# One written order for all nine chunks, and written places in SBUF and PSUM, for a local-attention and gated feed-forward kernel

## The chip, the cores and the metric

The kernel runs on one core of one Trainium2 chip, and the number that counts is the device time of one launch in microseconds. Before the change the median of three runs is 921.24 us (918.97, 921.24 and 921.79). One profiled execution was taken beside them; all rows quoted here are from it.

## The reference

The first half is attention of 8 batches with 8 heads of width 64: 512 local tokens that see the 32 global tokens and their neighbours within 32 places, and 32 global tokens that see all 544. The second half is a gated feed-forward layer on all 4608 tokens, with width 512 and hidden width 1536:

```python
a_l = sm(concat([s_lg, where(|i - j| <= 32, s_ll, -1e9)]));  out_l = a_l @ concat([v_g, v_l])
out_g = sm(scale * q_g @ concat([k_g, k_l]).T) @ concat([v_g, v_l])
x  = concat([out_g, out_l]).transpose(0, 2, 1, 3).reshape(4608, 512)
xn = x / sqrt(mean(x * x) + 1e-6) * rms_g
g, val = xn @ w_gate, xn @ w_val
out = (g * sigmoid(g) * val) @ w_out
```

## The kernel before, in words

The tokens are worked in nine chunks: chunks 0 to 7 are the 512 local tokens of a batch, chunk 8 the 256 global tokens of all batches. While TensorE (PE) does the feed-forward matmuls of one chunk, the attention of the next is done between them.

**Chunks 0 and 1** come first, with the weights still being made ready. `convert` (L451) loads a raw weight tile and splits it into two f16 parts on DVE and ACT, and chunk 0's feed-forward (`first_chunk`, L1747) waits for these tiles; its products with the first weights are jobs I, those with w_out are jobs O. The attention of both chunks is `local_unit` (L647): jobs L (load q and k), S (scores), M (minimum and exponent's argument, DVE), E (exponent, ACT), T (transposes), C (copies), A (product with v), X (normalise), Q (squares). Meanwhile `fold` (L1304, J, j, u, w) and `fold_out` (L1266) make sums of weight blocks and store them in DRAM (`wd`, `wa`, `wb`).

**Chunks 2 to 7** use those sums: `moe_pair` (L1360) does seven products of 2x2 blocks instead of eight, in the order 6, 1, 5, 7, 2, 3, 4, each 12 matmuls of 256 columns into a bank `pq`. Products 6, 1 and 5 begin banks; product 7 is added onto bank 6 once `s` was copied out of it, 2 onto 1, 3 onto 5 and 4 onto 6 again. So a product can wait for the DVE or ACT instruction (steps R) that read its bank. `moe_out` (L1547, O0 to O41) does the same with w_out into banks `pr`. Chunk 8 has plain `moe_f` products and `moe_out`. Attention is `local_halves` (L788, steps L, V, S, M, E, N, F, D, T, A, B, X, Y) and `global_unit` (L967): GS (scores), GM and GN (minimum and exponent), GT (transposes of the exponents `ge` into `gt`), GA (products). The weight tiles are read again for every chunk by `fetch` (L1339, tiles `wt`) and `fetch_out` (L1348, tiles `wu`): 512 KB each, on SP's DMA queue, which issues its transfers in order and waits at each until its buffer is free.

**Places.** SBUF tiles come from pools that rotate: tag "wf" has 12 buffers for `wt`, `wu`, `s`, `od` and the first weights, "wo" 7, "st" 6, "h" 6, "e" 4, "v" 4, "t" 3, "w" 3. The n-th tile of a tag takes the buffer of the n-12th (n-7th, ...), and waits for its readers. PSUM's eight banks are split the same way: "po" two, "pg" and "pv" one each, and four "pa" for attention (`attn_bank`, L446).

**Order.** All five engines are in a manual schedule (L1903): each runs its instructions as the program writes them. Chunk 0's jobs stand in a hand-made string ORDER (L40) and each is written out whole. For chunks 1 to 8 the instructions are recorded first and replayed in the order of a string per chunk, `_ORDER_1` to `_ORDER_8`, one chunk wholly behind the other. A piece "P12.0" is step P12's first run of instructions on one engine; a new piece begins where the engine changes, and at every instruction in steps R, t and n. Because replaying is done by a helper, every instruction of chunks 1 to 8 carries its line, L1929, in the profile:

```python
def write(engine, call):
    c, step, n, on = at_work
    if on and (on != engine or step[0] in "Rtn"):
        n += 1
...
for c, plan in plans.items():
    for name in orders.get(c, plan):
        for call in plan.pop(name) if c in orders else plan[name]:
            call()
```

Of the kernel before, what the change touches and what calls it, by code (L numbers as in the profile page):

```python
# [39 lines left out]
ORDER = """  # L40

# [22 lines left out]


_ORDER_1 = """
w0.0 S/0+1.0 M1/0+1.0 E1/0+1.0 w2.0 M3/0+1.0 E3/0+1.0 P0.0 N2/0+1.0 P1.0 N3/0+1.0 M2/0+1.0 E2/0+1.0
N1/0+1.0 M0/0+1.0 w3.0 w5.0 E0/0+1.0 N0/0+1.0 F0/0+1.0 P4.0 w6.0 F3/0+1.0 P5.0 R5.0 R6.0 P8.0 P9.0
F1/0+1.0 D1/0+1.0 R9.0 R1.0 F2/0+1.0 D3/0+1.0 D3/0+1.1 R10.0 P6.0 P7.0 R7.0 D0/0+1.0 D2/0+1.0
D2/0+1.1 R2.0 T2/0+1.0 P10.0 P11.0 w8.0 w9.0 P12.0 P2.0 T3/0+1.0 P3.0 D0/0+1.1 T0/0+1.0 D1/0+1.1  # L70
T1/0+1.0 A/0+1.0 B/0+1.0 P14.0 w12.0 Y/0+1.0 R3.0 R4.0 R5.1 w14.0 R11.0 R12.0 w1.0 X/0+1.0 R8.0 R9.1
GL/1+1.0 w15.0 P18.0 P16.0 P17.0 X/0+1.1 P19.0 Y/0+1.1 R17.0 R18.0 R19.0 R20.0 P13.0 R13.0 P32.0
P33.0 w18.0 GS/1+1.0 GM/1+1.0 Y/0+1.2 R13.1 GN/1+1.0 P24.0 P25.0 R14.0 w45.0 w20.0 w21.0 GM/1+1.1
GN/1+1.1 GT/1+1.0 GN/1+1.2 GT/1+1.2 GT/1+1.1 GT/1+1.3 P15.0 R15.0 L/2+1.0 S/2+1.0 R33.0 R34.0
M0/2+1.0 M2/2+1.0 N0/2+1.0 w49.1 N1/2+1.0 M3/2+1.0 N3/2+1.0 w24.0 E3/2+1.0 F3/2+1.0 P20.0 w17.0
R21.1 P40.0 D3/2+1.0 R25.0 R26.0 N2/2+1.0 R16.0 E2/2+1.0 R17.1 P21.0 R21.0 P22.0 P23.0 D3/2+1.1
R22.0 R23.0 T3/2+1.0 w26.0 w27.0 R24.0 R25.1 P26.0 P27.0 R27.0 R28.0 V/2+1.0 E0/2+1.0 F0/2+1.0
M1/2+1.0 F2/2+1.0 P28.0 P29.0 P41.0 R41.0 R29.1 X/0+1.2 w30.0 Y/0+1.3 P34.0 w23.0 P35.0 P30.0
D0/2+1.0 D0/2+1.1 R29.0 P31.0 R35.0 w44.0 P42.0 R30.0 R31.0 GV/1+1.0 R42.0 E1/2+1.0 GA/1+1.0 P43.0
F1/2+1.0 D1/2+1.0 D1/2+1.1 T1/2+1.0 w32.0 w33.0 L/0+2.0 R36.0 R37.1 P36.0 GD/1+1.0 P38.0 P66.0 R43.0  # L80
R44.0 D2/2+1.0 T0/2+1.0 D2/2+1.1 T2/2+1.0 w38.0 P37.0 R37.0 R38.0 w47.0 R45.1 w40.0 A/2+1.0 B/2+1.0
Y/2+1.1 X/2+1.0 X/2+1.1 w41.0 R32.0 P39.0 X/2+1.2 P44.0 P45.0 Y/2+1.0 X/2+1.3 Y/2+1.2 Y/2+1.3 R39.0
R40.0 R45.0 R46.0 R41.1 S/0+2.0 N0/0+2.0 M3/0+2.0 n53.0 P46.0 P47.0 n53.1 w46.0 R47.0 E3/0+2.0 n55.0
n55.1 n55.2 N1/0+2.0 n55.3 V/0+2.0 N2/0+2.0 n55.4 w48.0 n55.5 R33.1 N3/0+2.0 M2/0+2.0 E2/0+2.0
F2/0+2.0 P48.0 P67.0 P68.0 P49.0 P50.0 n55.6 n55.7 n55.8 n55.9 n55.10 w48.1 w35.0 P69.0 P70.0 n55.11
n55.12 n55.13 P51.0 P52.0 n56.0 R48.0 R49.0 P71.0 D2/0+2.0 M1/0+2.0 w46.1 n57.0 GX/1+1.0 w29.0
M0/0+2.0 D2/0+2.1 E0/0+2.0 n57.1 n64.1 w42.0 w49.0 w51.0 n65.0 P53.0 F3/0+2.0 n63.2 R71.0 w11.0
R53.0 F0/0+2.0 P54.0 P55.0 w54.0 w43.0 E1/0+2.0 F1/0+2.0 n56.1 n58.0 n58.1 R71.1 n62.1 n59.0 n59.2
P56.0 P57.0 D0/0+2.0 D0/0+2.1 n61.1 w56.0 P58.0 P59.0 n59.1 n63.0 P60.0 P61.0 GX/1+1.1 T2/0+2.0
w57.0 R53.1 D3/0+2.0 D3/0+2.1 D1/0+2.0 D1/0+2.1 T1/0+2.0 n64.0 n63.1 n60.0 n61.0 n65.1 T3/0+2.0  # L90
P62.0 P63.0 w59.0 P64.0 P65.0 R65.0 T0/0+2.0 R59.0 n62.0 R65.1 R59.1 n66.0
"""
# [187 lines left out]
def attention_moe_kernel(  # L280
# [363 lines left out]
    def local_unit(c, hp):  # L644
# [5 lines left out]
        def bank(name, tag):  # L650
            if not lead:
                return attn_bank(name)
# [1515 lines left out]
```

## Time and profile before

| | us |
|---|---|
| runs | 918.97, 921.24, 921.79 |
| span of the profiled execution, first to last instruction | 922.7 |
| PE busy | 878.8 (95%) |
| DVE busy | 724.5 (79%) |
| ACT busy | 556.3 (60%) |
| GpSimd (POOL) busy | 273.2 (30%) |
| mean granted TensorE clock | 0.980 of full speed |

The span is the profiled execution's own time; no other is given for it. It lies 1.46 us above the median of the runs. A busy time is the union of the times of an engine's instructions, so what is missing to the span is time in which the engine did nothing. In a list of waits each row is an engine's operation, what ended its idle time, the sum, the count and the longest. In the chain of waits each piece is a start, a duration and the engine and operation that the end of the program hung on at that moment.

### The profile page before, as it was taken

To read this page: it belongs to the slowest core of one execution; us is meant where nothing else is said; L and a number is where in the kernel's file an instruction comes from. 1 tells how busy PE (TensorE), PEld (TensorE's weight loads), DVE (VectorE), ACT (ScalarE), POOL (GpSimd) and SP (SyncE) were. 2 spreads that over 40 slices of the span, in tenths; PEclk is the share of its full clock that TensorE was granted. 3 is DMA by queue.
4 is the path that set the end of the run, shared out by engine and by line. 5 is a ranking of instruction groups with operands and counts; after the bars stand their busy time and mean duration, and the time that the engine had idled before them with its cause. 6 is when DMAs were issued, how large, how long until landed. Compare 5 with 4: busy or idle time off the path is not lost.

```text
span 922.7 us, 27756 instructions
## 1 busy us (share of the span) xinstructions
PE 878.8 (95%) x11430; PEld 671.4 (73%) x11430; DVE 724.5 (79%) x1831; ACT 556.3 (60%) x1341; POOL 273.2 (30%) x244
## 2 busy tenths in 40 slices
PE   5699989999999999999999999898999999999998
PEld 4644445544547886588888888787888888888887
DVE  6899998868796887877987888587887897777554
ACT  6899995636452755457565767466575862456132
POOL 0000000032435776306440244122520454133311
PEclk9699989999999999999999999999999999999999
DMA  9983615495377869686677769667876666888665
GB/s 337 405 301 106 192 47 173 130 333 174 90 248 243 274 206 300 194 257 233 206 258 263 245 222 293 198 208 243 265 250 223 206 222 244 247 246 273 215 232 191
DMA packets 101006, 212.03 MB, mean 230 GB/s; under 512 B 8080, under 2 KB 34448, under 8 KB 100880
## 3 DMA queue, kind: packets, MB, share of 16 engines
q1 hardware_dynamic: 100448, 209.94, 69.5%
q8 instruction: 89, 1.46, 0.6%
q10 hardware_dynamic: 432, 0.33, 0.1%
q14 instruction: 37, 0.30, 0.1%
HBM read 183.24 MB, written 27.00 MB: 228 GB/s over the span
## 4 chain that ended last, share of the span: by engine, by line
PE 40%; DVE 5%; DMA 3%; ACT 3%; issue 2%; POOL 1%; DVEq 0%; ACTq 0%; POOLq 0%; SPq 0%
PE pq L1929 20%; PE pr L1929 14%; PE p L1929 3%; DMA wt<-wd 2%; ACT e L1929 1%; PE a L1929 1%; DVE v L1929 1%; DMA wu<-wb 1%; DVE s L1929 1%; DVE u L1929 1%; POOL hs L1929 1%; POOL hu L1929 1%; PE s L1929 1%; ACT s L1929 1%; DVE t L1929 1%
## 5 line engine op out<-in xcount | busy, mean ns | idle before, releaser
L1929 PEld LDWEIGHTS <-wt 128*128 128x128 f16 x3312 | 322.7, 98 | 56.9 <-issue 11.1
L1929 PE MATMUL pq<-xh,wt 128*128 128x256 f16 x1152 | 206.6, 274 | 6.8 <-DMA wt<-wd 2.5
L1929 PE MATMUL pq<-ht,wt 128*128 128x256 f16 x1296 | 158.0, 274 | 2.1 <-POOL ht L1929 1.2
L1929 PE MATMUL pq<-xl,wt 128*128 128x256 f16 x576 | 157.8, 274 | 0.1
L1929 ACT ACTIVATE e<-e,sm 128x128 f32<-128x128 f32 x288 | 104.2, 390 | 27.8 <-DVE sm L1929 27.8
L1929 POOL TENSOR_TENSOR hu<-v,hu 128x256 f16<-128x256 f32 (+1 forms) x60 | 56.5, 958 | 177.6 <-ACT hu L1929 155.1
L1929 PE MATMUL pr<-wu,hs 128*128 128x256 f16 x792 | 92.4, 273 | 0.3 <-DVE hs L1929 0.3
L1929 POOL TENSOR_TENSOR e<-e,sm 128x512 f32<-128x512 f32 x24 | 27.7, 1162 | 205.3 <-DVE sm L1929 205.3
L1929 PEld LDWEIGHTS <-hs 128*128 128x128 f16 x792 | 77.4, 98 | 9.7 <-DVE hs L1929 0.6
L1929 POOL TENSOR_TENSOR hs<-u,hs 128x512 f16<-128x512 f32 x50 | 60.5, 1228 | 65.6 <-ACT hs L1929 37.9
L1929 PE MATMUL pr<-wu,hu 128*128 128x256 f16 x594 | 70.8, 273 | 1.0 <-DMA wu<-wb 0.6
L1929 DVE TENSOR_TENSOR s<-pq,s 128x512 f32<-128x512 f32 x66 | 44.9, 685 | 29.9 <-PE pq L1929 14.1
L1929 ACT ACTIVATE t<-u,half_inv 128x512 f32<-128x512 f32 x72 | 49.6, 717 | 27.0 <-DVE u L1929 23.0
L1929 DVE SCALAR_TENSOR_TENSOR t<-t,u 128x512 f32<-128x512 f32 x72 | 54.0, 758 | 14.4 <-ACT t L1929 14.3
L1929 ACT COPY s<-pq 128x512 f32<-128x512 f32 x72 | 41.3, 580 | 38.3 <-DVE s L1929 18.2
L1929 PEld LDWEIGHTS <-hu 128*128 128x128 f16 x594 | 57.6, 98 | 8.6 <-DMA wu<-wb 0.9
L1929 DVE TENSOR_TENSOR v<-pq,s 128x512 f32<-128x512 f32 x72 | 49.0, 683 | 18.6 <-PE pq L1929 14.8
L1929 PE MATMUL po<-wo,h 128*128 128x512 f16 x288 | 63.4, 379 | 0.0
L1651 PE MATMUL p<-xh,wf 128*128 128x512 f16 x192 | 58.8, 379 | 3.1 <-DVE t L1763 1.2
L1929 PE MATMUL p<-xh,wf 128*128 128x512 f16 x192 | 59.8, 385 | 0.5 <-DVE t L1929 0.5
L1651 PEld LDWEIGHTS <-wf 128*128 128x128 f16 x288 | 27.7, 98 | 37.0 <-issue 3.1
L1929 PEld LDWEIGHTS <-wf 128*128 128x128 f16 x288 | 27.8, 99 | 34.6 <-issue 2.9
(380 smaller groups left out, 1704.7 us busy)
## 6 DMA issues: line engine op xcount, KB each, us to landing
wt<-wd SPq DMA_DIRECT2D x120, 512.0 KB, 5.3
wu<-wb SPq DMA_DIRECT2D x36, 512.0 KB, 5.3
wr<-in_w_in_dram SPq DMA_DIRECT2D x24, 512.0 KB, 8.7
wu<-wa SPq DMA_DIRECT2D x24, 512.0 KB, 4.7
k<-in_qkb_dram SPq DMA_DIRECT2D x24, 448.0 KB, 6.5
gkq<-in_gkq_dram SPq DMA_DIRECT2D x16, 576.0 KB, 7.1
wt<-wd SPq DMA_DIRECT2D x36, 256.0 KB, 4.2
v<-in_vb_dram SPq DMA_DIRECT2D x24, 352.0 KB, 5.6
```

Of the source, the lines that this page charges most:

```text
L1651: nc.tensor.matmul(ps[:, :n], rows[:, a, o : o + P], ch[z][k][:, :n], start=(k == 0 and i == 0), stop=(k == NK - 1 and i == 2),)
L1929: return lambda *a, **k: write(self.engine, lambda: call(*a, **k))
```

## The change

Chunk 0 is now recorded like the others (`JOBS` only says which jobs there are), and one string ORDER of 3692 pieces "chunk:step.n" holds all nine chunks, so that steps of different chunks can be written in any order. Every instruction on DVE and GpSimd is now a piece of its own, in all chunks. No instruction goes to another engine, and the arithmetic and the transfers stay as they were.

The pools that rotate are gone. SBUF is 43 pages of 1024 words and 8 wide ones of 1152 words in each partition, allocated once, and PSUM is eight banks. A string PAGES names the page (and the quarter of it) of each of 1169 tiles, and a string BANKS the bank of each of 444 uses. Tiles under 256 words get a place of their own for the whole run. A tile's first writer now waits for the last readers of whatever the strings put in that place before it.

```diff
-for name in ORDER.split():
-    job.pop(name)()
-plans = {c: {} for c in range(1, NCH)}
-at_work = [1, "", 0, ""]
+plan = {}
+at_work = [0, "", 0, ""]
...
-        if on and (on != engine or step[0] in "Rtn"):
+        if on and (on != engine or engine in ("vector", "gpsimd") or c and step[0] in "Rtn"):
             n += 1
...
+for name in JOBS.split():
+    doing(0, name)
+    job.pop(name)()
...
-    orders = {c: names.split() for c, names in ORDERS.items()}
-    for c, plan in plans.items():
-        for name in orders.get(c, plan):
-            for call in plan.pop(name) if c in orders else plan[name]:
-                call()
+    for name in ORDER.split() or list(plan):
+        for call in plan.pop(name):
+            call()
...
+    page = [con.tile([P, 1024], F32, tag=f"page{i}", name=f"page{i}") for i in range(NPAGE)]
+    wide = [con.tile([P, 1152], F32, tag=f"wide{i}", name=f"wide{i}") for i in range(NWIDE)]
+    banks = [psum.tile([P, 512], F32, tag=f"bank{i}", name=f"bank{i}") for i in range(8)]
+    def tile_of(shape, dt, name):
+        n = int(np.prod(shape[1:])) * (2 if dt in (F16, BF16) else 4) // 4
+        if n < 256:
...
+            return con.tile(shape, dt, tag=tag, name=tag)
+        at = next(page_at)
...
+    def bank_of(name):
+        return banks[int(next(bank_at))]
...
-        t = pool.tile([P, 2, 2, 2, HT], F16, tag="wf", bufs=NF, name=f"wt{c}_{g}{i}")
+        t = tile_of([P, 2, 2, 2, HT], F16, f"wt{c}_{g}{i}")
...
-            ps = [[attn_bank(f"gs{b}{h}{z}") for z in range(2)] for h in range(2)]
+            ps = [[bank_of(f"gs{b}{h}{z}") for z in range(2)] for h in range(2)]
...
-    nc = bacc.Bacc("TRN2", target_bir_lowering=False, num_devices=1)
+    nc = bacc.Bacc("TRN2", target_bir_lowering=False, num_devices=1, dynamic_dma_scratch_size=2048)
```

The start of the order before, and after:

```
z0 L0 S0 M0.0 M0.1 L1 S1 M1.0 E0.0 M1.1 E0.1 T0.1 T0.0 W0 m0 s0 E1.0 C0.0 z1 l0 g0 L2 S2 M2.1 T1.0
0:L2.0 0:L0.0 0:S0.0 0:M0.0.0 0:M0.0.3 0:M0.0.1 0:M0.0.2 0:E0.0.0 0:z0.0 0:M0.1.2 0:L3.0 0:W1.0
```

## Rows read from the trace of the kernel before

**Rows 1.** The page: busy time of each engine.

```profile
PE 878.8 (95%) x11430; PEld 671.4 (73%) x11430; DVE 724.5 (79%) x1831; ACT 556.3 (60%) x1341; POOL 273.2 (30%) x244
```

**Rows 2.** Stages: start:end, length, PE, PEld, DVE, ACT, POOL busy, clock, DMA, GB/s.

```profile
0.00:44.10 44.10, 27.27 (x602) 23.54 (x603) 32.52 (x149) 34.00 (x100) 0.20 (x4) 0.77 0.98 370
44.10:129.10 85.00, 77.37 (x719) 39.48 (x719) 82.23 (x195) 81.49 (x141) 0.00 (x0) 0.98 0.54 183
129.10:172.40 43.30, 43.30 (x513) 24.22 (x511) 36.98 (x85) 26.69 (x66) 0.00 (x0) 0.97 0.32 109
172.40:910.50 738.10, 722.23 (x9528) 576.68 (x9523) 570.47 (x1401) 413.63 (x1034) 272.24 (x239) 0.99 0.73 236
910.50:922.70 12.20, 8.68 (x78) 7.53 (x78) 2.27 (x5) 0.48 (x2) 0.72 (x1) 1.00 0.27 101
```

**Rows 3.** Waits of PE from 129.1 us to the end: sum, times, longest.

```profile
PE pq L1929 <- DMA wt<-wd: 3.4, 4, 2.2
PE gt L1929 <- ACT ge L1929: 2.6, 2, 2.3
PE a L1929 <- issue: 2.4, 2, 2.2
PE pq L1929 <- DVE s L1929: 1.9, 4, 1.2
PE pq L1929 <- ACT u L1929: 1.5, 1, 1.5
PE pq L1929 <- POOL ht L1929: 1.2, 1, 1.2
PE pq L1929 <- DVE u L1929: 0.6, 1, 0.6
PE pr L1929 <- DMA wu<-wb: 0.6, 1, 0.6
```

**Rows 4.** Four stretches of 3.4 us, as rows 2: the granted clock beside matmuls done.

```profile
589.40:592.80 3.40, 3.40 (x18) 2.36 (x17) 0.30 (x1) 1.32 (x4) 0.00 (x0) 0.50 0.99 266
...
596.20:599.60 3.40, 3.40 (x34) 3.05 (x32) 1.36 (x4) 0.59 (x1) 0.00 (x0) 1.00 0.17 64
626.90:630.30 3.40, 3.16 (x15) 2.24 (x16) 0.31 (x1) 3.35 (x14) 0.51 (x1) 0.50 0.99 295
210.50:213.90 3.40, 3.40 (x34) 1.43 (x39) 0.86 (x3) 1.54 (x4) 0.00 (x0) 0.50 0.57 160
```

**Rows 5.** Chain of waits, two places: start us, us, what.

```profile
498.07 9.17 PE pq L1929 x84
...
621.09 2.43 POOL hs L1929 x2
623.53 3.56 DMA wt<-wd
627.14 8.27 PE pq L1929 x60
```

**Rows 6.** Timeline of PE, 583 to 588 us: [idle before <- releaser].

```profile
583.46 2.22 PE L1929 MATMUL a<-et,v 32*64 32x256 f32 x139
...
587.86 0.42 PE L1929 MATMUL a<-et,v 32*64 32x64 f32 x21 [2.18 <-issue]
```

**Rows 7.** The page: the DMA queue of instructions (packets, MB, share).

```profile
q8 instruction: 89, 1.46, 0.6%
```

**Rows 8.** Waits of SP's DMA queue, whole span: the largest.

```profile
SPq L1929 <- PE pq L1929: 142.3, 65, 9.9
```

**Rows 9.** Waits of PE, 0 to 129.1 us: the two largest.

```profile
PE x00t L1110 <- DVE dg L1104: 6.3, 1, 6.3
PE s L688 <- DMA k<-in_qk_dram: 6.1, 1, 6.1
```

**Rows 10.** Waits of DVE, 8 to 125 us: for PE's attention products.

```profile
DVE x L757 <- PE a L746: 2.2, 1, 2.2
```

**Rows 11.** DVE's t<-t,u, both inputs in SBUF: ns least/median/most.

```profile
L1929 DVE SCALAR_TENSOR_TENSOR t<-t,u x72: 650/685/1625, 298.3 to 847.8; 128x512 f32<-128x512 f32 x72
```

More of the change, by code (lines that the diff above doesn't have):

```diff
@@ L72 @@
[L72 to L77, printed above, removed]
@@ L645, in local_unit @@
         u = c * (H // 2) + hp
[L646 removed]
         st = {}
         xt = chunks[c]["x"]
[L650 to L664 removed]
+        def load():
+            q = tile_of([P, SL], F32, f"q{u}")
+            k = tile_of([P, 1024], F32, f"k{u}")[:, :KU]
             nc.sync.dma_start(q, qk[u, :, :SL])
@@ L669, in load_v @@
         def load_v():
-            tag = "wf" if lead and hp >= 2 else "v"
             v = st["v"] = [
-                pool.tile([P, 1024], F32, tag=tag, bufs=NF if tag == "wf" else 4, name=f"v{u}{i}")
+                tile_of([P, 1024], F32, f"v{u}{i}")
                 for i in range(2)
@@ L679, in scores @@
             q, k = st["q"], st["k"]
-            st["sm"] = pool.tile([P, 3, 8], F32, tag="sm", bufs=SMB, name=f"sm{u}")
-            ps = st["ps"] = [bank(f"s{u}{h}", "pa") for h in range(2)]
+            st["sm"] = tile_of([P, 3, 8], F32, f"sm{u}")
+            ps = st["ps"] = [bank_of(f"s{u}{h}") for h in range(2)]
             for i in range(NT):
@@ L769, in sums @@
             if hp == 0:
-                chunks[c]["ss"] = pool.tile([P, 4, NK], F32, tag="ss", name=f"ss{c}")
+                chunks[c]["ss"] = tile_of([P, 4, NK], F32, f"ss{c}")
             nc.vector.tensor_reduce(
@@ L794, in load @@
             if w == 0:
-                late["mask"] = con.tile([P, 6 * P], F32, tag="mask", name="maskb")
+                late["mask"] = tile_of([P, 6 * P], F32, "maskb")
                 nc.sync.dma_start(late["mask"], maskb)
@@ L864, in scores @@
         def scores():
-            st["sm"] = pool.tile([P, 3, 16], F32, tag="sm2", bufs=2, name=f"sm{u}")
-            ps = [[attn_bank(f"s{u}{x}{bk}") for bk in range(2)] for x in range(2)]
+            st["sm"] = tile_of([P, 3, 16], F32, f"sm{u}")
+            ps = [[bank_of(f"s{u}{x}{bk}") for bk in range(2)] for x in range(2)]
             st["s"] = ps
@@ L885, in scores @@
             st["et"] = [
-                pool.tile([P, 1088], F32, tag="k", name=f"et{u}{x}") for x in range(2)
+                tile_of([P, 1088], F32, f"et{u}{x}") for x in range(2)
             ]
@@ L909, in values @@
             if ms[0] == blocks[0]:
-                st["a"] = [attn_bank(f"a{u}{p}") for p in range(4)]
+                st["a"] = [bank_of(f"a{u}{p}") for p in range(4)]
             ps = st["a"]
@@ L931, in values, with taken @@
                         )
-        def take(z):
+        def taken(z):
             x = x_part(c, 2 * hp + z)
@@ L1231, in high @@
                 pair = [
-                    pool.tile([P, 512], F16, tag=s, bufs=4, name=f"{s}{c}{p}") for s in ("xh", "xl")
+                    tile_of([P, 512], F16, f"{s}{c}{p}") for s in ("xh", "xl")
                 ]
@@ L1362, in moe_pair @@
         st = {}
-        bank = {6: "po", 1: "pg", 5: "pv"}
+        own = (6, 1, 5)
         onto = {7: 6, 4: 6, 3: 5, 2: 1}
@@ L1367, in products @@
         def products(n, p):
-            if p in bank:
-                st["ps", p] = psum.tile(
-                    [P, 512], F32, tag=bank[p], bufs=2 if bank[p] == "po" else 1, name=f"pq{p}_{g}"
-                )
+            if p in own:
+                st["ps", p] = bank_of(f"pq{p}_{g}")
             ps = st["ps", p] = st["ps", onto.get(p, p)]
@@ L1374, in products @@
             hi, lo = ch["op"][p]
-            first = p in bank
+            first = p in own
             for j in range(2):
@@ L1513, in sums, with both @@
                 nc.vector.tensor_tensor(s[:, 1, 1], v[:, 1, 0], s[:, 0, 1], ALU.subtract)
-        def both(name, tag, bufs):
-            t = pool.tile([P, 2, 1024], F16, tag=tag, bufs=bufs, name=f"{name}{g}")
+        def both(name):
+            t = tile_of([P, 2, 1024], F16, f"{name}{g}")
             t = t[:, :, : 4 * w].rearrange("p a (j n) -> p a j n", j=2)
```

805 lines of the change are left out of this document (477 added, 328 removed), and 9 rows, old and new, of the table BANKS.

## The prediction

> **What bounds the kernel now.** I read the busy times first: TensorE (PE) is busy 878.8 us, DVE 724.5 [rows 1]. No matmul goes away, so the floor of any reordering is about PE's work, and only PE's idle time and its stretches at half clock can be won. The view by stage says where the idle time lies [rows 2]: 44.1 - 27.27 = 16.8 us before the first feed-forward matmul; 85.0 - 77.37 = 7.6 us up to chunk 0's first O product; nothing in the next 43.3 us; 738.1 - 722.23 = 15.9 us over chunks 1 to 8; 12.2 - 8.68 = 3.5 us in the tail, nearly all behind the last matmul. The first 129 us have another bound: DVE is busy 82.23 and ACT 81.49 of 85 us, making weights and attention ready [rows 2], so PE waits there because of work, not order.
>
> For the 15.9 us I read what ended PE's waits [rows 3]. No cause is large: weight tiles 3.4 + 0.6, the global units' exponents 2.6, no visible releaser 2.4, and copies out of a bank that the next product is added onto (s, u) 1.9 + 1.5 + 0.6, POOL 1.2. The eight rows hold 14.2 us. The stretches of 3.4 us show what they cost besides [rows 4]: with the granted clock at 1.00 (2.4 GHz) one did 34 matmuls, at 0.50 (1.2 GHz) one did 18, so it lost 16 x 0.10 = 1.6 us. There are three such stretches after 172 us, each behind a PE wait of over 2 us (210.5 follows the exponents' wait, 589.4 the one without releaser, 626.9 a weight tile's). What order can win in chunks 1 to 8 is thus 15.9 + 3 x 1.6 = 20.7 us.
>
> **The change part by part.** The sum is made against the profiled span of 922.7 us, 1.46 above the median of 921.24; I subtract from the median.
>
> *Weight tiles.* The chain shows how such a wait comes about [rows 5]: POOL's `hs` ended, only then SP issued the `wt` load into that buffer, 3.56 us later the product began, at half clock. The queue spends its time like this: 142.3 us of waiting for `pq` products alone [rows 8]. I counted in both orders the PE work between a tile's fetch and its first use, a 256-column matmul at 9.17/84 = 0.109 us [rows 5]. For `wt` of chunks 3 to 7 the mean grows from 8 to 13 us to 39 to 54 us, for `wu` from 4 to 11 us to 31 to 58 us. Tiles with under 8 us of lead fall from 109 to 31. Of 3.4 + 0.6 us I take off the share of those that go, 78 of 109: 2.9. With the half-clock stretch: -4.5 us. Bounds: -5.6 (all), and 0 if the page is not free when the fetch stands at the queue's head.
>
> *Exponents before their transposes.* GS to GT had 2.6 us of PE work in three of eight units, and now has 5.2 or more in all, up to 51. I take off 2.6 + 1.6 = -4.2 us; bounds -4.2 and -2.1 (one of the two waits stays).
>
> *The wait without releaser.* Before it PE ran 139 small matmuls, each with a weight load of its own, in 2.22 us, and then stood 2.18 us [rows 6]. The queue that carries instructions moved 89 packets of 1.46 MB / 89 = 16 KB [rows 7]; PE has 2 x 11430 instructions [rows 1], and 22860 / 89 = 257 of them a packet. So 278 instructions outran a packet here. The text of the change cannot show whether the boundaries now fall elsewhere: dense groups that stand side by side (A with B, GT with GT) number 12 before and 12 after. Bounds 0 and -(2.4 + 1.6) = -4.0; only one of 12 such groups stalled, so one cannot count on it either way: -2.0, the middle. [...]
>
> *Products added onto a bank.* The work between a product and the one onto its bank (144 pairs in chunks 2 to 7) grows from 4.4 to 6.4 us in the mean; the least is one product, 1.3 us, in both. DVE's s, ACT's u and DVE's u cost 4.0 us now; halved, -2.0. POOL's `ht` 1.2: halved, -0.6. Bounds 0 and -5.2.
>
> *Port.* DVE's t<-t,u takes 0.685 us but up to 1.625 [rows 11], only in operations with two SBUF inputs, as if POOL held it off. DVE is not the bound after 172 us (570 of 738 us busy [rows 2]), so calmer pieces gain nothing beyond the copies above: 0.
>
> *The first 129 us.* Unit 2's q and k are loaded ahead of unit 0's: 640 KB at the 370 GB/s of this stage [rows 2], 1.7 us, on top of the 6.1 us that the first scores wait for k [rows 9]; if the first scores are of unit 0, nearly all of it is paid. DVE's wait for attention products, 2.2 us [rows 10], can be covered by conversion work now that single instructions can be moved. DVE's work ahead of the first O product falls from 123.6 to 121.6 us, ACT's rises from 121.3 to 123.7. Conversion of one weight tile is moved ahead of the norm of chunk 0 (the 6.3 us at x00t [rows 9]), so that DVE's counted work ahead of the first feed-forward matmul rises from 37.0 to 40.4 us and ACT's from 38.6 to 42.2; it is spared later. I take 0; bounds -4 (both engines' savings) and +4 (load 1.7 and ACT's 2.4).
>
> *Chunk 0 to 1, tail.* PE is never idle from 129.1 to 172.4 us [rows 2]: a new mixture there gains 0. The tail hangs on the last product and its store: 0.
>
> *New waits.* The new order has its own least distances (31 short leads, 1.3 us between products). One stall like the weight tile's, 2.2 + 1.6 = 3.8 us, is what a single bad place costs; bounds 0 and, in this case, 3.8; I take half, +1.9.
>
> Sum: -4.5 - 4.2 - 2.0 - 2.0 - 0.6 + 0 + 1.9 = -11.4; 921.24 - 11.4 = 909.8 us.
>
> **The rivals.** *B, the whole idle time goes.* If every wait of chunks 1 to 8 and its half-clock stretch disappears (20.7) and DVE's 2.2 us at the start too, the time is 921.24 - 22.9 = 898. For it: the leads are four times as long; against it: the least distances did not change.
>
> *C, others take their place.* PE's waits are eight different causes of 0.6 to 3.4 us; take one off and the next engine is late: DVE does 570 us in the same 738. If long leads hold pages that attention needs, its waits grow as the weights' shrink, and the time stays at 921.
>
> *D, slower: SP's queue blocks.* The queue issues in order. An early fetch that waits for a page holds everything behind it, and behind it stand the 31 tiles with under 8 us of lead and the loads of q, k and v. The longest wait at `pq` is already 9.9 us [rows 8]. Each tile so held stalls PE by the 2.2 us of 627.14 and 1.6 us of half clock, 3.8 in all. Against the -11.4 three of them make no difference, from four it is slower (925.0), with six it is 932.6. Against it: a wait of the queue hurts only if it exceeds the lead of a tile behind it, and 78 of 109 short leads are gone.
>
> **How the numbers follow.** Forecast 909.8 with 0.50: its own ends come from the bounds: tiles and instruction wait in full and no new wait give 921.24 - 5.6 - 4.2 - 4.0 - 2.0 - 0.6 = 904.8; one exponent wait left (+2.1), the whole new stall (+1.9) and the start's +4 give 917.8. B has 0.15, C 0.14, D 0.21. A measurement of this kernel tells about 0.3% from no change, 918.5 to 924.0. Faster: A and B, 0.65; same: C, 0.14; slower: D, 0.21. The range runs from 899, at the upper edge of B, to 929, between four and six stalls of D; outside it lie about half of B and half of D, 0.2.
>
> **What would show it.** Right: PE's idle time over chunks 1 to 8 falls from 15.9 to about 7 us, the waits for `wt` and `gt` fall to under 1 us each, at most one stretch at clock 0.50 stands after 172 us, and the first O product begins within 4 us of 129.1. B: idle under 2 us. C: idle still near 15 us, with other names. D: waits of PE for `wt` or `wu` of over 2 us, four or more, behind long waits in SP's queue. The forecast is wrong as a whole if the first stage ends later than 134 us or earlier than 124, for then DVE and ACT's order mattered, which I priced at nothing.

## The result and the profile after

The changed kernel takes 904.52 us (median of four runs, 902.98 to 905.86) against 920.29 us of the kernel before on the same chip: a ratio of 0.9821 with a 95% interval from 0.9802 to 0.9841, 15.8 us less. The two profiled executions are 922.7 and 903.1 us long, 19.6 us apart. The one of before was a long one. In the 48 other executions of that kernel that were timed beside the runs below, the time is 2.1 to 2.2 us more than the span, so the time of this one was some 924.8 us (an estimate): about 3.6 us above the median of 921.24, and not 1.46 as the span alone makes it. Its mean granted clock is 0.980, where those 48 have 0.987 in the median. The one of after is near its median (904.84 us, span 903.1, clock 0.989). So what is read from this pair can be up to some 4 us more than what the medians show.

Since tiles are now parts of pages, the names of tiles in the profile after are `page`, `wide` and `bank`, and the helper's line is L2088. The page of the kernel after, busy time of each engine (it answers to [rows 1]):

```profile
PE 869.2 (96%) x11430; PEld 668.4 (74%) x11430; DVE 701.2 (78%) x1831; ACT 553.8 (61%) x1341; POOL 273.8 (30%) x244
```

The same count of instructions on every engine, and PE is busy 9.6 us less: it does the same matmuls for less time at half clock (mean granted clock 0.989, before 0.980). The stages of after [rows 2], cut at its own first O product (123.2 us) and its own last stretch:

```profile
44.10:123.20 79.10, 78.34 (x748) 42.69 (x749) 77.93 (x184) 78.35 (x138) 0.00 (x0) 0.98 0.63 222
123.20:892.00 768.80, 760.99 (x10045) 600.34 (x10045) 591.23 (x1501) 441.62 (x1104) 271.33 (x235) 1.00 0.70 231
892.00:903.10 11.10, 7.56 (x69) 6.47 (x67) 2.58 (x7) 0.95 (x2) 2.26 (x5) 1.00 0.12 47
```

The kernel before from its first O product to the same matmul near the end:

```profile
129.10:910.50 781.40, 765.53 (x10036) 600.90 (x10034) 607.45 (x1485) 440.31 (x1100) 272.24 (x239) 0.99 0.71 229
```

So the 19.6 us are two pieces. Up to the first O product 129.10 - 123.25 = 5.9 us are won. From there to the end 13.7 us are won, 8.0 us of PE's idle time (from 15.9 to 7.8 us up to the last stretch, 3.5 us in both last stretches) and 5.7 us of PE's own. The last stretch of after is shorter only because the cut leaves it 69 matmuls, and that of before 78. PE's own 5.7 us go with the clock: no stretch at 0.50 is left behind 123 us in this execution. The kernel before had four behind 128 us: three are in [rows 4], the fourth, and one more ahead of it, are these:

```profile
121.80:125.10 3.30, 3.30 (x128) 2.89 (x112) 2.10 (x14) 3.30 (x11) 0.00 (x0) 0.50 0.03 5
128.60:132.00 3.40, 3.40 (x11) 1.50 (x10) 3.33 (x7) 2.80 (x6) 0.00 (x0) 0.50 0.18 71
```

How many such stretches there are differs from execution to execution (the mean granted clock of the 48 lies between 0.980 and 0.993), as the section on half clock below shows too, so the 5.7 us cannot be put down to the order alone.

The waits of PE in the kernel after, from the first O product on, answer to [rows 3]:

```profile
PE bank L2088 <- issue: 5.4, 7, 1.1
PE bank L2088 <- ACT page L2088: 1.3, 3, 0.6
PE bank L2088 <- DVE nt L2088: 0.4, 2, 0.3
PE bank L2088 <- POOL page L2088: 0.4, 1, 0.4
PE bank L2088 <- DVE sm L2088: 0.2, 1, 0.2
```

The reader is to see what is missing: no wait for a transfer, none for exponents. What is left has no visible releaser, and no wait is longer than 1.1 us. In the first stage the two waits of [rows 9] still stand; the one for k is longer (8.6 us, before 6.1):

```profile
PE bank L2088 <- DMA page<-in_qk_dram: 8.6, 1, 8.6
PE bank L2088 <- DVE page L2088: 6.8, 2, 6.6
```

### The profile page after: what moved, and what is told of

It reads as the page before. It is cut to its first block, busy times and chain, and to the rows that moved or that the text cites. A ratio compares the mean times of both kernels' runs of the same rounds, so it can differ in the third digit from the quotient of the medians.

```text
span 903.1 us, 27864 instructions
## 1 busy us (share of the span) xinstructions
PE 869.2 (96%) x11430; PEld 668.4 (74%) x11430; DVE 701.2 (78%) x1831; ACT 553.8 (61%) x1341; POOL 273.8 (30%) x244
## 3 DMA queue, kind: packets, MB, share of 16 engines
q8 instruction: 89, 1.46, 0.7%
## 5 line engine op out<-in xcount | busy, mean ns | idle before, releaser
L2088 PE MATMUL bank<-page,page 128*128 128x256 f16 (+6 forms) x8212 | 714.6, 281 | 24.8 <-DMA page<-in_qk_dram 8.6
L2088 PEld LDWEIGHTS <-page 128*128 128x128 f16 (+1 forms) x5472 | 525.0, 98 | 175.5 <-issue 11.4
L2088 POOL TENSOR_TENSOR page<-page,page 128x512 f16<-128x512 f32 (+5 forms) x177 | 200.5, 1152 | 361.4 <-ACT page L2088 319.8
L2088 ACT CAST page<-page 128x512 f16<-128x512 f32 (+1 forms) x156 | 121.2, 797 | 93.4 <-DVE page L2088 72.5
L2088 ACT COPY page<-bank 128x512 f32<-128x512 f32 (+3 forms) x163 | 85.1, 543 | 115.7 <-PE bank L2088 103.1
L2088 DVE TENSOR_TENSOR page<-bank,page 128x512 f32<-128x512 f32 x155 | 104.7, 685 | 59.2 <-PE bank L2088 48.7
L2088 ACT ACTIVATE page<-page,sm 128x128 f32<-128x128 f32 x352 | 128.8, 389 | 24.4 <-DVE sm L2088 21.7
L2088 DVE TENSOR_TENSOR page<-page,page 128x256 f32<-128x256 f32 (+5 forms) x171 | 102.4, 609 | 11.0 <-ACT page L2088 8.7
L2088 PE MATMUL bank<-wide,page 32*64 32x96 f32 (+6 forms) x2268 | 103.5, 271 | 1.3 <-issue 1.3
L2088 POOL TENSOR_TENSOR page<-page,sm 128x512 f32<-128x512 f32 x24 | 27.9, 1176 | 214.4 <-DVE sm L2088 200.5
L2088 ACT ACTIVATE page<-page 128x512 f32<-128x512 f32 (+2 forms) x94 | 77.6, 894 | 10.2 <-DVE page L2088 5.5
L2088 PEld LDWEIGHTS bank<-page,page 64*32 64x32 f32 (+4 forms) x3232 | 58.4, 116 | 29.5 <-issue 14.7
L2088 DVE CUSTOM_DVE_ANT_0 page<-bank,page 128x128 f32<-128x128 f32 x256 | 62.0, 284 | 19.9 <-PE bank L2088 16.5
L2088 DVE TENSOR_TENSOR page<-page 128x256 f32<-128x256 f32 (+3 forms) x127 | 69.3, 556 | 1.2
L2088 DVE SCALAR_TENSOR_TENSOR page<-page,page 128x512 f32<-128x512 f32 x65 | 46.9, 734 | 12.6 <-ACT page L2088 12.4
L2088 DVE SCALAR_TENSOR_TENSOR page<-page,c_h,page 128x512 f32<-128x512 f32 x69 | 51.7, 769 | 0.9
L2088 ACT ACTIVATE page<-page,half_inv 128x512 f32<-128x512 f32 x65 | 44.6, 716 | 12.8 <-DVE page L2088 11.5
L2088 ACT ACTIVATION_READ_ACCUMULATOR page<-page,sm 128x1 f32 x256 | 48.0, 187 | 0.0
L2088 PE MATMUL bank<-page,wide 128*128 128x256 f16 x330 | 41.7, 273 | 0.6 <-ACT page L2088 0.6
L2088 ACT ACTIVATE page<-bank,half_inv 128x512 f32<-128x512 f32 (+1 forms) x36 | 21.7, 610 | 31.7 <-PE bank L2088 31.7
L2088 DVE STREAM_TRANSPOSE wide<-page 128x512 f32<-128x512 f32 x48 | 32.6, 696 | 6.5 <-POOL page L2088 6.5
L2088 PEld LDWEIGHTS <-wide 128*128 128x128 f16 x330 | 31.9, 98 | 5.1 <-issue 1.0
```

The lines of the kernel that those rows point to most:

```text
L2088: return lambda *a, **k: write(self.engine, lambda: call(*a, **k))
```

## The experiments

Each run has its own kernel before on the same chip; ratios are to that.

### What sets the first O product

The chain to the first O product goes through the scale of w_out (steps K), which needs all six of its weights converted on DVE and ACT. The order before had eight pieces of chunk 0's hidden values ahead of it (c4 to c7, casts on ACT, and r4 to r7, subtractions on DVE), the new order has them behind. Here they are put back, and one page is changed so that they fit:

```diff
-0:K0.1 ... 0:c4.0 0:c5.0 0:c6.0 0:O0.1.0 ... 0:c7.0 ... 0:r5.0 ... 0:r4.0 0:r7.0 ... 0:r6.0
+0:c4.0 0:r4.0 0:c5.0 0:r5.0 0:c6.0 0:r6.0 0:c7.0 0:r7.0 0:K0.1 ... 0:O0.1.0
```

> The changed kernel with c4 to c7 and r4 to r7 of chunk 0 (ACT's casts and DVE's subtractions for the hidden values of 4 to 7) put ahead of the norm of w_out (step K0's second piece), as the order before had them. Theory DVE (what DVE and ACT have to do ahead of the last weights' scale sets the first O product): 4 x 0.69 us on DVE come ahead, so the first O product begins 2 to 3 us later (125.2 to 126.3 us), and the end as much, 906 to 908 us. Rival PE (the first O product came sooner because transposes and products of the attention no longer stand in a row in front of it): it begins within 0.7 us of 123.25 and the time stays within 1 us.

906.78 us, ratio 0.9859 (0.9827 to 0.9892). Timeline of PE in this run:

```profile
123.62 0.59 PE L2088 MATMUL bank<-kk,ones 128*128 128x1 f32 x2 [2.86 <-DVE kk L2088]
...
128.10 1.49 PE L2088 MATMUL bank<-page,page 128*128 128x512 f16 x3
```

and of the changed kernel at the same place:

```profile
120.35 0.28 PE L2088 MATMUL bank<-kk,ones 128*128 128x1 f32 x2
...
123.25 1.02 PE L2088 MATMUL bank<-page,page 128*128 128x512 f16 x4 [0.15 <-ACT page L2088]
```

DVE in this run, ahead of the scale's first step (`qo`):

```profile
119.43 1.29 DVE L2088 TENSOR_TENSOR wide<-page,wide 128x512 f16<-128x512 f32 x2 [0.73 <-ACT wide L2088]
120.64 1.29 DVE L2088 TENSOR_TENSOR page<-page,page 128x512 f16<-128x512 f32 x2
121.85 0.16 DVE L2088 TENSOR_TENSOR qo<-hs 128x6 f32<-128x6 f32 x1
```

The four subtractions and the wait for ACT's cast ahead of them take 0.73 + 2.42 = 3.15 us, and the matmul of the scale, which waits 2.86 us for DVE's `kk`, comes 3.3 us later than in the changed kernel. The first O product comes 4.9 us later, more than expected: behind the wait the clock was 0.50 for two stretches, so that the way from the scale to the O product took 4.5 us in place of 2.9. In the kernel before the scale's matmul came 4.9 us later than in the changed one:

```profile
125.25 0.38 PE L626 MATMUL nrm<-kk,ones 128*128 128x1 f32 x2
```

So the eight pieces are 3.3 of those 4.9 us; what the rest is, no run shows. For the first O product the theory DVE holds, with half clock on top. The end moved less, by 3.6 us between the profiled executions (906.7 and 903.1 us) and by 2.3 between the medians, and the intervals of the two ratios overlap.

The loads of unit 0 ahead of those of unit 2:

```diff
-0:L2.0 0:L0.0 0:S0.0
+0:L0.0 0:L2.0 0:S0.0
```

> The changed kernel with the loads of unit 0 ahead of those of unit 2 again. Theory: the first scores begin 1.7 to 2.5 us sooner (6.1 to 6.9 us in place of 8.6) and, since DVE is packed from there to the first O product, that product and the end come 1.5 to 2.5 us sooner: 901.5 to 903 us. Rival: unit 2's scores are the ones that DVE then waits for, and the first O product stays within 0.7 us of 123.25.

902.80 us, ratio 0.9816 (0.9788 to 0.9844): 1.7 us less than the changed kernel and in the range of the theory, but the intervals overlap. The first O product came at 120.89 us, 2.4 us sooner, as the theory has it, and the profiled execution ended 2.0 us sooner (901.1 us). Near 515 us a new wait stands:

```profile
515.68 4.57 PE L2088 MATMUL bank<-page,page 128*128 128x256 f16 x25 [2.62 <-DMA page<-wd]
```

The tile was issued at 511.87, because SP's queue had waited for a store:

```profile
SPq L2088 <- PE bank L2088: 10.8, 3, 5.3
SPq L2088 <- DMA out_dram<-page: 5.5, 1, 5.5
```

and the clock fell behind it:

```profile
516.50:519.90 3.40, 3.40 (x19) 2.38 (x17) 0.59 (x2) 0.68 (x1) 2.64 (x3) 0.51 0.20 74
```

The page of this weight tile had held an output tile, and the load could not start until the store of that tile was through. So one of 1169 places was changed on top of the loads:

```diff
-24a 7c 20a w2 w1 27a 29a 10c W5a W4a 22a 15a 15c 1a 4a W4a 11a 0a 15a 4c 24a 28a 25a 11a 36a 23a 4a
+24a 7c 20a w2 w1 27a 29a 10c W5a W4a 22a 15a 15c W2a 4a W4a 11a 0a 15a 4c 24a 28a 25a 11a 36a 23a 4a
```

> The run with unit 0 loaded first, and one page changed: the weight tile of chunk 4 that TensorE waited 2.6 us for there (its page held an output tile, so SP waited 5.5 us for that tile's store to land) goes to wide page 2, which is free for long. Theory QUEUE (that one wait and the stretch at clock 0.50 behind it gave back the 2.4 us that the earlier start had won): no wait of TensorE for wd over 1 us, no stretch at 0.50 after 172 us, 898 to 901 us. Rival: the 2.4 us are lost elsewhere, 901.5 to 904 us.

901.03 us, ratio 0.9774 (0.9754 to 0.9794), 3.5 us less than the changed kernel and the fastest of this study. The wait is gone (all waits for `wd` after 123 us: 0.7 us), no stretch at 0.50 is left behind 172 us, so the theory QUEUE holds for the cause of that wait. Its price is not shown: the first O product lay at 122.1 us in this execution and the span was 900.2 us, the median is 1.8 us below that of the run before it and just above what was expected, and the intervals of the two ratios touch. Nor had the wait given back the whole 2.4 us, since that run had already ended 2.0 us sooner than the changed kernel.

### Leads and distances, as the prediction counted them

The fetches of 162 pieces were moved back to about 9 us of PE work ahead of their use, for example

```diff
-6:w52.0 7:w11.0 8:w48.0 6:t43.1
+6:w52.0 7:w11.0 6:t43.1
...
-8:R48.4 8:R50.0 8:O12.0
+8:R48.4 8:R50.0 8:w48.0 8:O12.0
```

> The changed kernel with each fetch of a weight tile for chunks 3 to 8 moved back in the order to about 9 us of TensorE work ahead of its first use (162 pieces moved; the mean lead was 44 us). Theory LEADS (long leads are what took the weight tiles' waits away): waits of TensorE for the loads come back, 3 to 6 us in all, with at least one stretch at clock 0.50 after 172 us; 908 to 913 us. Rival: with the new order of the other steps and the new places 9 us are enough: within 2 us of the changed kernel, waits for loads under 1 us.

902.66 us, ratio 0.9825 (0.9786 to 0.9864): no loss. The waits of PE behind 123.8 us have no weight tile among them:

```profile
PE bank L2088 <- issue: 2.5, 3, 1.3
PE bank L2088 <- DMA page<-in_qkb_dram: 1.5, 2, 1.3
```

The time between a fetch's issue and its first use, matched tile by tile, tells why. For chunks 3 to 8 its mean by chunk is 12 to 18 us in the kernel before, 48 to 63 us after, and 17 to 27 us here; but tiles with under 7 us are 36 before, 5 after and 4 here. So the rival holds for a mean of 17 to 27 us, and what lies above that is surplus. The leads of before were not put back by this run: moved back in the order, the fetches still went out sooner on the clock than in the kernel before. That the few short leads decide, and with them when their places come free, is argued from the counts.

The exponents' transposes were put back close behind the scores:

```diff
-1:GN/1+1.2 1:R15.0 ... 1:P21.0 ... 1:GT/1+1.0 ... 1:P22.0 1:GT/1+1.2
+1:GN/1+1.2 1:GT/1+1.0 1:GT/1+1.2 1:R15.0 ... 1:P21.0 ... 1:P22.0
```

> The changed kernel with the transposes of global unit 0's exponents (GT, two runs of five matmuls) put back behind the same 2.6 us of TensorE work after its scores as in the order before, in place of 6.5 and 10.5 us; two banks are changed so that they fit. Theory EXPONENTS (the longer way between GS and GT is what took away the wait of 2.34 us and the stretch at clock 0.50 behind it): a wait of TensorE of 1.5 to 2.6 us at the first GT, near 200 us, and a stretch at 0.50 behind it; 907 to 909.5 us. Rival (DVE and ACT reach the exponents sooner in the new order anyway): under 0.7 us there, 903.5 to 905.5 us.

903.82 us, ratio 0.982 (0.976 to 0.988). The wait is 0.39 us:

```profile
202.01 1.49 PE L2088 MATMUL bank<-ident,wide 128*112 128x128 f32 x10 [0.39 <-ACT wide L2088]
```

So the distance was not the cause, and the theory EXPONENTS falls. The timeline of DVE in the kernel before shows another one:

```profile
206.89 0.44 DVE L1929 CUSTOM_DVE_ANT_0 ge<-gs,zeros 128x272 f32<-128x272 f32 x1 [3.34 <-DMA wd<-wq]
```

DVE could not write the exponents' tile because its buffer still held a sum of weights that a store was reading. The kernel before was run with a buffer of its own for `ge` and its order as it was. With that the tiles behind `ge` in tag "st" take other buffers than before, and the scratch space for DMA is smaller; no run took these apart:

```diff
-            e = pool.tile([P, 1152], F32, tag="st", bufs=ST, name=f"ge{b}")
+            e = pool.tile([P, 1152], F32, tag="ge", bufs=1, name=f"ge{b}")
...
-    nc = bacc.Bacc("TRN2", target_bir_lowering=False, num_devices=1)
+    nc = bacc.Bacc("TRN2", target_bir_lowering=False, num_devices=1, dynamic_dma_scratch_size=2048)
```

> The kernel before, with one place changed: the exponents ge of the global units get a buffer of their own instead of the next of the six of tag st (the scratch space for DMA is set to 2048 so that it fits, as in the changed kernel). Theory PLACE (the first GT waited 2.34 us because DVE could not write ge until the store of wq, the last tile in that buffer, had been read out): DVE no longer waits 3.3 us for a store near 206 us, TensorE's wait at that GT is under 0.7 us, and no stretch at clock 0.50 follows it; 2 to 4 us less than the kernel before in the same call (ratio 0.9955 to 0.998). Rival ORDER (2.6 us between GS and GT are too few under any place): a wait of 1.5 us or more stays.

915.61 us, ratio 0.9949 (0.9928 to 0.9969), 4.2 us less. The transposes run without a wait and the clock stays at 1.00 there:

```profile
204.60 1.26 PE L1929 MATMUL gt<-ident,ge 128*112 128x128 f32 x10
```

The theory PLACE holds: with another buffer the wait is gone. The gain (2.9 to 6.6 us by the interval) agrees with the wait of 2.34 us and a stretch at half clock behind it, 3.9 us.

### Places

The order of after with 605 of its 1169 pages dealt anew at random, each to one that is free for the tile's whole life in the order:

```diff
-3a 0c 2a 0c 3c 10a 2a 10a 3c 13a 1a 16a 16a 0a 1a 4c 11a 12a 0a 24a 4a 5a 23a 10c 4a 6a 7a 14a 19a
+3a W0a 33a 6a 17c 15c 28a W6a 41c 36a 21a 5a 10a 28a 9a W6c 14a 11a 41c 33a W2c 14a 24a 16c 24c 38a
...
```

> The changed kernel with its order untouched and 605 of the 1169 pages dealt anew at random, each to a place that is free for the tile's whole life in the order (banks as they were). Theory PLACES (an order alone is not enough; which reader a fetch must wait for decides when SP's queue can issue it): waits of TensorE for transfers come back, 5 us or more in all, with stretches at clock 0.50; 909 to 925 us. Rival: any places that fit the order do, 903 to 907 us.

969.24 us, ratio 1.0511 (1.0490 to 1.0533): 65 us more than the changed kernel, and far more than expected. The waits of PE behind 123 us:

```profile
PE bank L2089 <- DMA page<-wd: 13.8, 4, 7.5
PE bank L2089 <- DVE page L2089: 10.9, 7, 5.9
PE bank L2089 <- DVE wide L2089: 4.8, 3, 3.2
PE bank L2089 <- DMA page<-wb: 4.3, 1, 4.3
```

Transfers and DVE are late alike, and thirteen stretches of 3.4 us at 0.50 stand behind 240 us, where the changed kernel has none (mean clock 0.966 against 0.989). Only pages differ, so an order alone is not enough, and the theory PLACES holds, at a price far above what it had. That a writer is late because its page still has a reader on another engine, and holds back what stands behind it in its queue, is the reading here; it was not followed tile by tile.

The order of before in the pages and banks of after, each tile in the free place left longest ago:

```diff
-0:L2.0 0:L0.0 0:S0.0 0:M0.0.0 0:M0.0.3 0:M0.0.1 0:M0.0.2 0:E0.0.0 0:z0.0 0:M0.1.2 0:L3.0 0:W1.0
+0:z0.0 0:L0.0 0:S0.0 0:M0.0.0 0:M0.0.1 0:M0.0.2 0:M0.0.3 0:M0.1.0 0:M0.1.1 0:M0.1.2 0:M0.1.3 0:L1.0
...
```

> The order of the kernel before, piece by piece, in the pages and banks of the changed kernel; each tile gets the free place that was left longest ago. Theory ORDER (the gain comes from what stands where in the order): about the time before, 917 to 923 us (ratio 0.996 to 1.002); the first O product begins between 127 and 131 us, and TensorE still waits for weight tiles, 3 us or more in all. Rival PLACES (the gain comes from buffers that are free sooner, so that loads start sooner under any order): 912 us or less (ratio 0.991 or less), waits for weight tiles under 1 us.

942.79 us, ratio 1.0247 (1.0212 to 1.0282): slower than the kernel before, which neither theory had. Its first O product came at 130.3 us, close to the 129.1 of before, so the gain at the start belongs to the order. Behind that my places cost more than the rotating buffers. One wait of PE, and SP's queue ahead of it:

```profile
362.26 2.15 PE L2089 MATMUL bank<-page,page 64*32 64x128 f32 x69 [2.70 <-DMA page<-in_qkb_dram]
```
```profile
341.94 1.02 SPq L2089 DMA_DIRECT2D wb<-page  x2
353.94 1.77 SPq L2089 DMA_DIRECT2D page<-in_qkb_dram  x4
```

The load of q stood 11 us at the head of the queue, until matmuls had read what was in its page, and all that followed stood behind it. That is the mechanism of rival D, in another kernel. Order and places cannot be judged apart: each is made for the other.

### Instruction packets

64 matmuls of one column, ahead of the first scores where PE waits for k anyway, move every later instruction of PE by 128 places (each matmul has a weight load: the page counts 11430 of both). A packet is taken as 256 instructions, an estimate: the prediction counts 257 from [rows 1] and [rows 7], and the places of the waits, as told below, repeat every 128 matmuls:

```diff
+    for _ in range(64):
+        nc.tensor.matmul(banks[7][:2, 0:1], one16[:, 0:2], one16[:, 0:1], start=True, stop=True)
     nc = Written
```

In the kernel before (into a bank of its own, `first`):

> The kernel before, with 64 matmuls of one column (two instructions each with their weight load) put ahead of the first scores, where TensorE waits for k anyway: every later instruction of TensorE moves by 128 places, half a packet of 256. Theory PACKETS (the wait of 2.18 us without a releaser stands where a dense run of small matmuls meets the end of a packet): the wait of over 2 us at the matmul that was number 7365 of the trace goes (under 0.5 us there) and others, at other places, come; the time moves by what goes and comes, 916 to 923 us. Rival LOAD (it comes from something else at this place, such as the transfers of that moment): it stands at the same matmul with 1.5 us or more.

930.16 us, ratio 1.0080 (1.0049 to 1.0111). The dense run that had stopped for 2.18 us after 139 matmuls [rows 6] now goes through, and another one stops:

```profile
191.77 0.62 PE L1932 MATMUL a<-et,v 32*64 32x64 f32 x35
196.41 0.30 PE L1932 MATMUL a<-et,v 32*64 32x32 f32 x3 [4.02 <-issue]
...
587.36 2.38 PE L1932 MATMUL a<-et,v 32*64 32x256 f32 x160
```

In the changed kernel:

> The changed kernel with the same 64 matmuls ahead of the first scores. Theory PACKETS: the order was made for the old boundaries, so waits without releaser appear at other matmuls of dense runs, at least one of them over 1.2 us, 6 to 10 us in all after 123 us, with or without a stretch at clock 0.50; 904 to 909 us. Rival (the boundaries do not matter for this order): the waits stay at numbers 2764 and 5445 plus 64 and the time within 1.5 us of 904.5.

928.69 us, ratio 1.0069 (1.0046 to 1.0092): 24 us more than without the 64, and slower than the kernel before. The first O product still came at 124.7 us. Behind it the waits of PE are

```profile
PE bank L2088 <- issue: 20.3, 10, 5.1
PE bank L2088 <- ACT page L2088: 0.6, 2, 0.5
```

The longest of them, and the same run of matmuls in the changed kernel:

```profile
289.93 2.38 PE L2088 MATMUL bank<-wide,page 32*64 32x256 f32 x153
297.45 0.43 PE L2088 MATMUL bank<-wide,page 32*64 32x32 f32 x7 [5.14 <-issue]
```
```profile
284.28 2.40 PE L2088 MATMUL bank<-wide,page 32*64 32x256 f32 x160
286.61 5.42 PE L2088 MATMUL bank<-page,page 128*128 128x256 f16 x48
```

Both theories had too little here. The waits are 14.9 us more than without the 64, and five stretches at 0.50 stand behind 123 us, where the changed kernel has none (mean clock 0.978 against 0.989); at 1.6 us each (an estimate from [rows 4]) these are 8 us more. To tell the place in the packet from the extra matmuls, twice as many were put there, 256 instructions:

```diff
-    for _ in range(64):
+    for _ in range(128):
```

> The changed kernel with 128 matmuls of one column ahead of the first scores, twice as many as in the run with 64: TensorE's instructions move by 256, one whole packet. Theory PACKETS: every later instruction has the place in its packet that the order was made for, so the 20 us of waits without releaser go again: 903 to 907 us, such waits after 123 us 2 to 6 us in all, none over 1.5 us. Rival (the extra matmuls themselves, or any move at all, do it): 924 us or more.

902.96 us, ratio 0.9827 (0.9789 to 0.9865), and waits without releaser of

```profile
PE bank L2088 <- issue: 3.2, 5, 1.1
```

A whole packet more changes nothing that is clear of noise, half a packet costs 24 us. And 16 in place of 64, an eighth of a packet:

> The changed kernel with 16 such matmuls, which moves TensorE's instructions by 32, an eighth of a packet. Theory PACKETS says that the time lies between the changed kernel and the run with 64; with dense runs of 139 to 278 instructions most boundaries stay outside them: 905 to 915 us. Rival (the order fits only its exact places): 920 us or more.

911.56 us, ratio 0.9917 (0.9888 to 0.9946), with one wait of 3.29 us at 173.9 us inside a run of 64x128 scores, and 9.4 us of such waits in all. The theory PACKETS holds in all four runs for what goes and comes; its price was too low in the two with 64 matmuls. In the run with the old order in new pages it shows too: there a wait of 2.22 us stands at the same matmul of the sequence, to one record, as the 2.18 us of the kernel before, 15 us later on the clock.

The numbers of the matmuls agree with packets as well. In the traces of the kernels before and after, of these four runs and of the old order in new pages, every wait without releaser of over 0.7 us behind 123 us stands at a matmul whose number, counted from 0, leaves between 58 and 81 when it is divided by 128 (128 matmuls with their weight loads are 256 instructions), and the remainder falls slowly along the stream. Matmul 1871 leaves 79 (1.09 us in the changed kernel, 3.29 us with 16 more ahead), 1999 leaves 79 (1.14 us with 128 more), 5446 leaves 70 (2.75 us with 64 more), 7365 leaves 69 (2.18 us before). So the places where PE can stall stay in the stream; the matmuls ahead of the first scores change which of the dense runs meet them.

That PE waits there for a packet, no row names; the times speak for it. In the traces of the kernels before and after, the queue of [rows 7] moves 89 packets of 16384 bytes each, and from one to the next PE starts 127 (before) and 126 (after) matmuls in the mean, with their weight loads 254 and 253 instructions. The waits without releaser of over 0.7 us behind 123 us are one before and five after, and each of the six ends 1.3 to 1.5 us after such a packet landed: the one of 2.18 us ends at 587.86, the packet landed at 586.52.

## Why the prediction was right, and where not

**The whole.** 909.8 us was forecast, 904.5 measured, inside the range. The gain is 15.8 us against the kernel before on the same chip (16.7 against the 921.24 of the forecast), and 11.4 were forecast. By its own signs the forecast was right in part: PE's idle time over chunks 1 to 8 fell to 7.8 us, the waits for weight tiles and exponents are gone, and no stretch at 0.50 stands after 172 us. But the first O product was to stay within 4 us of 129.1, and its start at 123.25 us is earlier than the 124 us at which the prediction calls itself wrong as a whole, "for then DVE and ACT's order mattered, which I priced at nothing". It did matter. That the time still lies in the range is in part luck: 5.9 us came where nothing was priced, and about 9.9 us are left by the medians for the part that was priced at 11.4. Rival C is out. Rival B's idle time under 2 us did not come (7.8 us are left). Rival D did not come in this kernel, but such a stall is real: the run with unit 0's loads first had one, of 2.62 us.

**The first 129 us: the step that failed.** It is the sentence that PE waits there "because of work, not order", and with it the term of 0 with bounds of 4 us either way; the first O product came 5.9 us sooner. I had counted DVE's work ahead of it (123.6 to 121.6 us) and balanced it with ACT's, but did not ask which of it lies ahead of the one step that all O products need, the scale of w_out. The run e_r_early shows that eight pieces there are worth 3.3 us up to the scale and 4.9 us up to the first O product, partly by the clock: the stretches at 0.50 at 121.8 and 128.6 us were not in my sum. The 1.7 us for the load of unit 2 were too little: the first scores began 2.5 us later, and putting the loads back won 2.4 us up to the first O product.

**Chunks 1 to 8: the size was about right, three of its reasons were not.** Forecast -11.4; from the first O product on -13.7 between the two profiled executions, and about -9.9 by the medians.

- *Weight tiles* (-4.5): the waits of 4.0 us and their stretch at half clock are all gone. But I argued from the mean lead in the order, and the run that cut it to less than half on the clock lost nothing. What is left as a reason is the few short ones, and that these hang on places; no run took that by itself, but the random pages brought 18 us of waits for weight tiles under the same order.
- *Exponents* (-4.2): gone too, and confirmed as a size by the run of the kernel before with one buffer changed (-4.2 us, between -2.9 and -6.6). The cause that I named, too little work between GS and GT, was refuted; the buffer was the cause. Following the wait one step further back, from ACT to DVE to the store, would have shown it.
- *The wait without releaser* (-2.0): its sum rose from 2.4 to 5.4 us; what went was only its length and the half clock behind it. That it comes from packets of instructions agrees with the four runs that moved them and with the landings above. I treated it as a lottery over 12 places, while order and boundaries fit each other in both kernels: moved by half a packet, such waits add up to 20 us here, and the kernel before loses 0.8% too. Inside a dense run of small matmuls up to 5.14 us stood open (f_shift).
- *Products onto a bank* (-2.0, and -0.6 for POOL): the waits for `s`, `u` and `ht` were 5.2 us, and 1.3 + 0.4 us are left behind ACT and POOL, where the rows no longer tell the tiles. No run took this part by itself, so that the longer distance did it is argued only.
- *DVE beside POOL* (0): of the 72 `t<-t,u` in the trace of before, the 57 with no POOL instruction beside them took 0.650 to 0.693 us, and all that took longer, up to 1.625, had one; `v<-pq,s`, with one input in PSUM, took 0.650 to 0.692 in both cases. So the reading of [rows 11] stands. DVE is busy 701.2 us, before 724.5, and no run took this part by itself.
- *New waits* (+1.9): no new wait over 1.1 us came.

**Half clock.** I counted three stretches after 172 us, each behind a wait of over 2 us, as something that goes with its wait, and put 3 x 1.6 us of them into what order can win. The run of the kernel before with one buffer changed (r_before_ge) has two of these waits at the same two matmuls,

```profile
582.57 0.42 PE L1929 MATMUL a<-et,v 32*64 32x64 f32 x21 [2.05 <-issue]
...
620.33 0.28 PE L1929 MATMUL pq<-xh,wt 128*128 128x256 f16 x1 [2.35 <-DMA wt<-wd]
```

and its clock stayed at 1.00 behind both; its profiled execution has no stretch at 0.50 behind 124 us (span 914.5 us, mean clock 0.989). So a wait of 2 us is not followed by one every time. A mean clock of 0.980 against 0.987 in the median points to more of them in the execution that I read than in the usual one, and I took their price off the median. The rate of [rows 4] shows in single matmuls too: at 1.00, f16 matmuls of 256 and of 512 columns start 0.109 and 0.216 us apart in the trace of before, at 0.50 they start 0.213 and 0.427 us apart. So 256 columns more take 0.107 and 0.214 us: 2.4 and 1.2 columns per ns, an estimate from these times, and that is what the trace shows for the 2.4 and 1.2 GHz of the prediction. That one stretch costs about 1.6 us agrees with that run's gain (4.2 us for a wait of 2.34), but its interval, 2.9 to 6.6 us, does not test it closely.

## What to carry to other kernels

A distance in the written order is not a lead on the clock (about 9 us in the order were 17 to 27 us on the clock in c_short_leads): ask for each late load or late writer which buffer it writes, who read that last (a store counts as a reader: it held `ge` back for 3.34 us), and what stands behind it in its queue. Ahead of a stage that waits for one step, sort the work of the bounding engines by whether that step needs it, not by its sum. And where an engine runs many short instructions, ask where its dense runs meet the end of a packet of instructions (here about 256 of them, by the count and by the run that moved PE by 256 and kept its time), and put them so that they end before it (no run here did only that); whoever adds or removes instructions ahead of them has to time the rest anew, since here 128 more instructions cost more than the whole change had won.

## What was not expected of the hardware

The place of a dense run in the stream of instructions is worth up to 24 us of 904 (half a packet), 7 us (an eighth) and nothing (a whole packet). In the run with 64 extra matmuls the waits of over 1 us there are 1.0 to 5.1 us each, the longest at 297.45 us. And pages that are free by the order, dealt anew at random, cost 65 us with no instruction added or moved.
